# Attention followed by a squared-ReLU layer: where the score scale is applied, and which engine empties the value products

## The chip, the cores and the metric

The kernel runs on one core of one Trainium2 chip. The metric is the device time of one execution in microseconds; before the change it is 1281.25 us (median of 3 runs, 1281.09 to 1282.95). The engines are TensorE (PE for matmuls, PEld for its weight loads), VectorE (DVE), ScalarE (ACT), GpSimd (POOL) and SyncE (SP, which issues nearly all DMAs here). Each runs its own list of instructions in order; they meet through semaphores.

## What is computed

```python
# q, k, v: (8 batches, 8 heads, 576, 64), fp32; tau = 0.02
scores = (1 / 8) * q @ k.T
thresh = max(scores, axis=-1) - tau
scores = where(scores >= thresh, scores, -1e9)
attn   = exp(scores - max(scores, axis=-1))
attn   = attn / (sum(attn, axis=-1) + 1e-9)
x      = attn @ v                       # then (B, H, S, D) -> (4608, 512)
h      = maximum(x @ w_in, 0)           # w_in: (512, 2048), handed over as float64
out    = (h * h) @ w_out                # w_out: (2048, 512), float64 too
```

## The kernel before

The first 0.49 ms are attention, the rest the two matmuls of the feed-forward layer, which the change does not touch.

**Tiling of attention.** Two heads make a pair; there are 32 pairs. A *unit* is 128 rows of queries (or the two 64-row rests of two pairs) for both heads of a pair against all 576 keys; there are 144 units. The program runs in 72 *periods* (`period(p)`, p from -2 to 74, of which the outer ones are partial). Each scores and normalizes two units, A = 2p and B = 2p + 1, and multiplies the weights of the two units of p - 2 with the values.

**Operands.** Queries and keys are loaded by rows, turned by TensorE into PSUM (`turn`, L399; step `T`) and copied from there to SBUF by ScalarE (step `eT`). For an even turn these are a pair's 512 main queries (`qT`, two pieces of 256), for an odd one its 576 keys (`kT`, a piece of 256 and one of 320) and its 64 rest queries (`qR`). The pieces of queries are scaled on the way: the copy is an activation whose scale is the column `qscale` (L413). `qscale` is -1/8 in each partition, made from tau (L119), so that the scores come out negated and the maximum is a minimum. A pair is turned every second period: 62 turns fall on 62 periods, and of the periods from 3 on 14, 23, 32, 41, 50, 59 and 68 to 71 have none.

**One period.** The steps are written as lists of words (`PLAIN`, `CONVERTING`, `FIRSTS`, L606 to L622); each word issues its instructions, and so the list sets every engine's own order. Periods 3 to 34 use `CONVERTING`, since there the float64 weights are also taken apart into fp32 (c1 to c6, on ScalarE, VectorE and GpSimd); periods 35 to 71 use `PLAIN`; periods 0 to 2 have lists of their own. The words that matter:

- `SA`, `SB`: scores of A and B (L445), for each of 2 heads and 2 halves of 64 rows a matmul of 512 keys and one of the remaining 64, into PSUM.
- `topA1`, `topA0`, `topB1`, `topB0` (L463, VectorE): one maximum pass for each head. It reads 576 scores from PSUM, multiplies by 1.0, writes them to SBUF and gives their minimum in a second, small instruction (the accumulator's readout).
- `leastA`, `leastB` (L470, GpSimd): threshold; `powA1` and so on (L473, ScalarE): the exponential; `maskA1` and so on (L478, VectorE): the exponential times the comparison of the score with the threshold, which is a column with one value for each partition, and the sum.
- `over` (L485, GpSimd), `inv` (L488, VectorE), `spread` (L528, GpSimd): the reciprocal of the sums, widened for a transpose.
- `V`, `W`, `U` (L388): transposes of the weights; `eV`, `eW`, `eU` (L535, ScalarE): their copies to SBUF. `V` and `U` share one PSUM tile.
- `PV` (L544): the value products, 72 matmuls, into PSUM banks 0 (head 0) and 5 (head 1).
- `x` (L665, L667): VectorE multiplies head 0's product by the reciprocals on the way to SBUF, ScalarE copies head 1's; `xs` (L682): GpSimd multiplies head 1's by the reciprocals, and SP writes both to DRAM.

**Banks.** The scores fill PSUM banks 0 to 5. A's lie in banks 0, 1 and 4, 5, B's in 1, 2 and 3, 4. So `PV` follows A's two maximum passes, `T` (banks 1 and 4) follows B's, and the next `SA` follows `x` and `eT`. These waits between engines are worked out by `touch` (L363).

The plain list, which sets the order in the second half of attention:

```python
PLAIN = """
    fetch U SA topA1 over s1 topA0 SB topB1 inv sV eU powA1 idE V topB0 leastA spread PV powA0
    maskA1 leastB maskA0 eV T powB1 x maskB1 powB0 xs maskB0 eT W eW
""".split()
```

Of the kernel before, what the change touches and what calls it, by code (L numbers as in the profile page):

```python
# [10 lines left out]
FP32 = mybir.dt.float32  # L11
I32 = mybir.dt.int32
U32 = mybir.dt.uint32
ALU = mybir.AluOpType
# [34 lines left out]
def kernel(  # L49
# [25 lines left out]
    nc = tc.nc  # L75
    B, H, S, D = q.shape
    P = 128
# [260 lines left out]
    def places(i):  # L338
        if i not in turned:
            turned[i] = (  # L340
                sb.tile([P, MAIN], FP32, tag="qT", bufs=Q_RING, name="qT"),
                sb.tile([P, S], FP32, tag="kT", bufs=K_RING, name="kT"),
                sb.tile([P, REST], FP32, tag="qR", bufs=K_RING, name="qR"),
            )
        return turned[i]

# [52 lines left out]
    def turn(i, which, spots, other=None):  # L399

        nat, to = loaded.pop((i, which)), places(i)
        of = [nat[:, t, :] for t in range(FULL)] + ([loaded.pop((i, 2))] if which else [])
        for t, x in enumerate(of):
            for r, (spot, at) in enumerate(spots):
                rows = ds(r * HALF, HALF)
                made = nc.tensor.transpose(spot[:, ts(t, HALF)], x[rows, :], ident[rows, rows])  # L406
                touch("turns", made, at, BANK)
        half = FULL * HALF

        kind = "turned k" if which else "turned q"  # L410

        def scaled(to, spot):
            touch(kind, nc.scalar.activation(out=to, in_=spot[0], func=AF.Identity, scale=qscale[:, :]), spot[1], BANK, i)  # L413

        def then():
            part = lambda r, x, n: (spots[r][0][:, ds(x, n)], spots[r][1])
            if which:
                for r, n in ((0, half), (1, half + REST)):
                    spot = part(r, 0, n)
                    copy_by = other if r and other else nc.scalar.copy  # L420
                    touch(kind, copy_by(to[1][:, ds(r * half, n)], spot[0]), spot[1], BANK, i)
                scaled(to[2], part(0, half, REST))
                next_keys(i)
            else:
                for r in range(2):
                    scaled(to[0][:, ds(r * half, half)], part(r, 0, half))
                for n in later_loads(i, 0):
                    load_q(n)

        return then  # L430

# [2 lines left out]
    def scores(n, rest):  # L434

        of, t = units[n]
        at_k, count = (MAIN, REST) if rest else (0, MAIN)
        for j in range(2):
            first = n % 2 != j
            to = (3 * j + 1) * BANK + first * (BANK - REST) if rest else (3 * j + 2 * first) * BANK  # L440
            for c in range(2):
                rows, at = ds(j * D, D), ds(c * HALF, HALF)
                qT, kT, qR = turned[of[c]]
                lhs = qT[rows, ds((c * FULL + t) * HALF, HALF)] if t < FULL else qR[rows, :]
                made = nc.tensor.matmul(  # L445
                    sc[at, ds(to, count)], lhs, kT[rows, ds(at_k, count)], start=True, stop=True
                )
                touch("q scores" if t < FULL else "scores", made, to, count, of[c])

    def softmax(n):  # L450

        if n % 2 == 0:
            smalls[n // 2] = sb.tile([P, 4, 4], FP32, tag="small", bufs=4, name="small")
        small = smalls[n // 2]
        nmx, thr, sm = (small[:, i, ds(n % 2 * 2, 2)] for i in range(3))
        w = sb.tile([P, CH, 2, D], FP32, tag="w", bufs=4, name="w")
        s = sb.tile([P, 2, S], FP32, tag="s", bufs=2, name="s")
        weights[n] = w
        of = lambda j: s[:, j, :].rearrange("p (c d) -> p c d", d=D)

        def top(j):
            at = 3 * j * BANK + (n % 2 != j) * (2 * BANK - REST)
            made = nc.vector.tensor_scalar(  # L463
                out=s[:, j, :], in0=sc[:, ds(at, S)], scalar1=1.0, scalar2=None,
                op0=ALU.mult, op1=ALU.min, accum_out=nmx[:, j : j + 1],
            )
            touch("tops", made, at, S)

        def least():
            nc.gpsimd.tensor_scalar(out=thr, in0=nmx, scalar1=tau_p[:, :], scalar2=None, op0=ALU.add)  # L470

        def power(j):
            nc.scalar.activation(  # L473
                out=w[:, :, j, :], in_=of(j), func=AF.Exp, bias=nmx[:, j : j + 1], scale=-1.0
            )

        def mask(j):
            nc.vector.scalar_tensor_tensor(  # L478
                out=w[:, :, j, :], in0=of(j), scalar=thr[:, j : j + 1], in1=w[:, :, j, :],
                op0=ALU.is_le, op1=ALU.mult, accum_out=sm[:, j : j + 1],  # L480
            )

        def over():
            sm = small[:, 2, :]
            nc.gpsimd.tensor_scalar(out=sm, in0=sm, scalar1=1e-9, scalar2=None, op0=ALU.add)  # L485

        def inverse():
            nc.vector.reciprocal(out=small[:, 3, :], in_=small[:, 2, :])  # L488

        soft[n] = dict(top=top, least=least, power=power, mask=mask, over=over, inverse=inverse)  # L490
# [140 lines left out]
    def period(p):  # L631
# [26 lines left out]
        def given_out():  # L658
            if has(2 * m):
                x = sb.tile([P, 2, P], FP32, tag="x", bufs=2, name="x")  # L660
                by_vector = (0,)
                for j in range(2):
                    by = sc[:, ds(5 * j * BANK, P)], wT[m][:, ts(SCALE_AT + j, P)]
                    if j in by_vector:
                        made = nc.vector.tensor_tensor(out=x[:, j, :], in0=by[0], in1=by[1], op=ALU.mult)  # L665
                    else:
                        made = nc.scalar.copy(x[:, j, :], by[0])  # L667
                    touch("x", made, 5 * j * BANK, P, m)
                late["x"] = x, [j for j in range(2) if j not in by_vector], wT[m]
                wT.pop(m)  # L670
                valued(m)

        def scaled_x():
            if has(2 * m):
                x, js, by = late["x"]
                if len(js) == 2:
                    nc.gpsimd.tensor_tensor(
                        out=x[:, :, :].rearrange("p j q -> p (j q)"), in0=x[:, :, :].rearrange("p j q -> p (j q)"),
                        in1=by[:, ds(SCALE_AT * P, 2 * P)], op=ALU.mult,
                    )  # L680
                for j in js if len(js) == 1 else ():
                    nc.gpsimd.tensor_tensor(out=x[:, j, :], in0=x[:, j, :], in1=by[:, ts(SCALE_AT + j, P)], op=ALU.mult)  # L682
                give_x(m, x)
            ask(False)

# [669 lines left out]
```

## Time and profile before

| | |
|---|---|
| median of 3 runs | 1281.25 us |
| span of the profiled execution | 1278.6 us |
| attention, about | 0 to 493 us of the span |
| granted TensorE clock | 1.000 |
| PE busy | 1255.2 us (98%) |
| DVE busy | 1000.2 us (78%) |
| ACT busy | 855.6 us (67%) |
| POOL busy | 897.4 us (70%) |

In the profile's rows, a form such as `128x576 f32<-128x576 f32` is partitions by elements, out from in; `x288` is the count; behind `|` stand the busy time in us, the mean of one instruction in ns, and the idle time just before such instructions with the engine and line that ended it. In a timeline a row has start, duration, engine, line and operation; several like instructions in a row are merged (`x2`), and idle time before them stands in brackets. The records of ScalarE and VectorE overlap, since an instruction's record begins before the one in front has ended: the time that one takes from its engine is read from start to start, not from its duration.

### The profile page before, as it was taken

The page shows a single profiled execution, that of the slowest core. Times are in us where ns is not written, and L with a number is a line of the kernel's source. Part 1 is how long each engine was busy: PE and PEld are TensorE (multiplying, and loading weights), DVE is VectorE, ACT ScalarE, POOL GpSimd, SP SyncE. Part 2 cuts the span into 40 slices and gives each one's busy share as a digit, 9 for nine tenths or more (in the row PEclk, how much of TensorE's full clock was granted, in tenths as well). Part 3 has the DMA queues.
Part 4 walks back from the last instruction along what each step waited for, and adds up shares of the span by engine and source line. Part 5 has one row for each costly group of instructions (what it writes and reads, how often), then busy time and mean ns, then how long its engine had stood idle before and what let it go on. Part 6 is the DMA issues. An engine that isn't in the chain of part 4 may idle for free.

```text
span 1278.6 us, 44201 instructions
## 1 busy us (share of the span) xinstructions
PE 1255.2 (98%) x17459; PEld 1087.0 (85%) x17459; DVE 1000.2 (78%) x2449; ACT 855.6 (67%) x1552; POOL 897.4 (70%) x1094
## 2 busy tenths in 40 slices
PE   8999999999999999999999999999999999999998
PEld 6666666677777768988888888999999999999998
DVE  6999999999999997787878877877645664565463
ACT  6999999999999995666765767667422441343240
POOL 2565665655555557888798889858877777786775
PEclk9999999999999999999999999999999999999999
DMA  6566666544333413457666666589635414522511
GB/s 155 152 158 160 165 193 182 151 94 112 89 83 84 97 34 98 156 164 219 198 190 204 192 198 187 177 324 394 208 122 166 133 50 149 166 95 76 161 35 34
DMA packets 256591, 191.89 MB, mean 150 GB/s; under 512 B 96000, under 2 KB 217344, under 8 KB 256384
## 3 DMA queue, kind: packets, MB, share of 16 engines
q1 hardware_dynamic: 254928, 188.63, 49.8%
q8 instruction: 137, 2.24, 0.7%
q14 instruction: 70, 0.57, 0.1%
q10 hardware_dynamic: 1456, 0.44, 0.1%
HBM read 116.65 MB, written 72.35 MB: 148 GB/s over the span
## 4 chain that ended last, share of the span: by engine, by line
PE 70%; DMA 1%; ACT 1%; DVE 1%; issue 1%; ACTq 0%; DVEq 0%; SPq 0%
PE po L1085 30%; PE ph L946 27%; PE sc L544 5%; PE sc L445 4%; PE pt L388 2%; DMA wall<-w 1%; PE sc L406 1%; PE sc L388 1%; DVE arena L128 1%; DVE arena L463 0%; DMA g<-arena 0%; ACT arena L916 0%; ACT c L879 0%; DMA arena<-xT 0%; ACT arena L917 0%
## 5 line engine op out<-in xcount | busy, mean ns | idle before, releaser
L128 POOL TENSOR_TENSOR arena<-arena 128x512 f32<-128x512 f32 (+1 forms) x314 | 377.7, 1222 | 126.3 <-DVE arena L128 89.4
L1085 PE MATMUL po<-wall,arena 128*128 128x128 f32 x3528 | 394.4, 275 | 0.2 <-DVE arena L125 0.2
L1085 PEld LDWEIGHTS po<-wall,arena 128*128 128x128 f32 x3528 | 394.1, 192 | 0.4 <-DVE arena L125 0.4
L946 PE MATMUL ph<-arena,wall 128*128 128x128 f32 (+1 forms) x2352 | 387.4, 327 | 1.1 <-DVE arena L665 0.5
L946 PEld LDWEIGHTS ph<-arena,wall 128*128 128x128 f32 x2352 | 354.2, 191 | 34.2 <-DVE arena L128 2.2
L128 DVE TENSOR_TENSOR arena<-ph,arena 128x512 f32<-128x512 f32 x378 | 255.6, 688 | 75.8 <-PE ph L946 50.0
L125 POOL TENSOR_TENSOR arena<-arena 128x128 f32<-128x128 f32 (+2 forms) x314 | 255.2, 814 | 29.1 <-DMA arena<-w 10.7
L879 ACT COPY c<-arena 128x512 f32<-128x512 f32 (+2 forms) x319 | 176.1, 558 | 104.2 <-DVE arena L125 85.7
L473 ACT ACTIVATE arena<-arena 128x576 f32<-128x576 f32 x288 | 232.1, 918 | 16.7 <-DVE arena L463 16.7
L128 DVE TENSOR_TENSOR arena<-po,arena 128x128 f32<-128x128 f32 x378 | 108.3, 290 | 168.0 <-PE po L1085 167.4
L478 DVE SCALAR_TENSOR_TENSOR arena<-arena 128x576 f32<-128x576 f32 x288 | 225.5, 811 | 0.4 <-POOL arena L470 0.4
L463 DVE TENSOR_SCALAR_CACHE_REDUCE arena<-sc 128x576 f32<-128x576 f32 x288 | 204.5, 751 | 14.3 <-ACT arena L535 6.4
L125 DVE TENSOR_TENSOR arena<-arena,c 128x512 f32<-128x512 f32 (+2 forms) x283 | 176.8, 633 | 7.9 <-ACT c L879 6.1
L544 PEld LDWEIGHTS sc<-arena 64*64 64x64 f32 x5760 | 144.4, 133 | 43.1 <-DVE arena L463 39.1
L445 PE MATMUL sc<-arena 64*64 64x64 f32 (+1 forms) x2304 | 170.0, 415 | 0.3 <-DVE arena L665 0.3
L544 PE MATMUL sc<-arena 64*64 64x128 f32 (+1 forms) x5760 | 160.8, 262 | 8.5 <-DVE arena L463 5.8
L535 ACT COPY arena<-pt 128x1024 f32<-128x1024 f32 x144 | 166.0, 1153 | 1.6 <-PE pt L388 1.5
L769 ACT COPY arena<-po 128x128 f32<-128x128 f32 x63 | 16.6, 264 | 185.4 <-PE po L1085 185.4
L388 PEld LDWEIGHTS pt<-ident,arena 64*128 64x128 f32 x2304 | 83.0, 138 | 41.7 <-ACT arena L535 33.8
L388 PE MATMUL pt<-ident,arena 64*128 64x64 f32 x2304 | 100.8, 227 | 2.4 <-ACT arena L535 2.1
L445 PEld LDWEIGHTS sc<-arena 64*64 64x64 f32 x2304 | 62.5, 132 | 47.5 <-issue 22.7
L470 POOL TENSOR_SCALAR arena<-arena,tau_p 128x2 f32<-128x2 f32 x144 | 65.5, 455 | 41.8 <-DVE arena L463 35.2
(51 smaller groups left out, 936.6 us busy)
## 6 DMA issues: line engine op xcount, KB each, us to landing
g<-arena SPq DMA_DIRECT2D x144, 256.0 KB, 2.6
arena<-g SPq DMA_DIRECT2D x144, 256.0 KB, 4.5
w<-arena SPq DMA_DIRECT2D x60, 256.0 KB, 2.8
wall<-w SPq DMA_DIRECT2D x49, 256.0 KB, 5.3
arena<-w SPq DMA_DIRECT2D x44, 256.0 KB, 3.1
arena<-in_v_dram SPq DMA_DIRECT2D x32, 288.0 KB, 4.6
out_dram<-arena SPq DMA_DIRECT2D x70, 128.0 KB, 2.4
arena<-in_q_dram SPq DMA_DIRECT2D x64, 128.0 KB, 4.1
```

The source lines that it names most:

```text
L125: e.tensor_tensor(out=out, in0=x, in1=y, op=ALU.subtract)
L128: e.tensor_tensor(out=out, in0=x, in1=y, op=ALU.add)
L388: made = nc.tensor.transpose(pt[:, r, ts(slot, HALF)], of[rows, :], ident[rows, rows])
L445: made = nc.tensor.matmul(sc[at, ds(to, count)], lhs, kT[rows, ds(at_k, count)], start=True, stop=True)
L463: made = nc.vector.tensor_scalar(out=s[:, j, :], in0=sc[:, ds(at, S)], scalar1=1.0, scalar2=None, op0=ALU.mult, op1=ALU.min, accum_out=nmx ...
L473: nc.scalar.activation(out=w[:, :, j, :], in_=of(j), func=AF.Exp, bias=nmx[:, j : j + 1], scale=-1.0)
L478: nc.vector.scalar_tensor_tensor(out=w[:, :, j, :], in0=of(j), scalar=thr[:, j : j + 1], in1=w[:, :, j, :], op0=ALU.is_le, op1=ALU.mult, a ...
L535: touch("weights", nc.scalar.copy(joined(to), whole(pt, 0, count)), at, 2 * BANK, m)
L544: made = nc.tensor.matmul(sc[ds(u * D, D), ds(5 * j * BANK + row, count)], loaded_v[i][rows, (c - (u != j)) % CH, :], wT[m][rows, ds(weigh ...
L879: nc.scalar.copy(c, y)
L946: nc.tensor.matmul(to[:, j, :], W_IN[m, k][:, ts(h * parts_ + j, P)], x_of(m, k), start=(not more and j == 0), stop=True, skip_group_check ...
L1085: nc.tensor.matmul(to, g[:, j, :], w[:, j, :], start=(not more and j == 0), stop=(j == 3), skip_group_check=True)
```

## The change

The scale leaves the copies of the turned queries. Queries and keys are copied plainly; the 64 rest queries now lie behind the first 256 keys in `kT`, so that an odd turn is copied in two pieces of 320. The scores in PSUM are plain products, and the maximum pass multiplies them by the column `qscale` in place of the constant 1.0. The keys in `kT` are no longer in one run: a score matmul of 512 keys reads two runs of 256, 320 apart.

Both value products are copied to SBUF by ScalarE, and GpSimd scales both with one instruction of 256 columns; VectorE has no part in it any more.

```diff
@@ -338,9 +338,8 @@
     def places(i):
         if i not in turned:
             turned[i] = (
-                sb.tile([P, MAIN], FP32, tag="qT", bufs=Q_RING, name="qT"),
-                sb.tile([P, S], FP32, tag="kT", bufs=K_RING, name="kT"),
-                sb.tile([P, REST], FP32, tag="qR", bufs=K_RING, name="qR"),
+                sb.tile([P, 2, FULL * HALF], FP32, tag="qT", bufs=Q_RING, name="qT"),
+                sb.tile([P, 2, (FULL + 1) * HALF], FP32, tag="kT", bufs=K_RING, name="kT"),
             )
         return turned[i]
 
@@ -405,27 +404,16 @@
                 rows = ds(r * HALF, HALF)
                 made = nc.tensor.transpose(spot[:, ts(t, HALF)], x[rows, :], ident[rows, rows])
                 touch("turns", made, at, BANK)
-        half = FULL * HALF
-
-        kind = "turned k" if which else "turned q"
-
-        def scaled(to, spot):
-            touch(kind, nc.scalar.activation(out=to, in_=spot[0], func=AF.Identity, scale=qscale[:, :]), spot[1], BANK, i)
+        kind, n = "turned k" if which else "turned q", (FULL + (1 if which else 0)) * HALF
 
         def then():
-            part = lambda r, x, n: (spots[r][0][:, ds(x, n)], spots[r][1])
+            for r, copy_by in enumerate((nc.scalar.copy, other or nc.scalar.copy)):
+                touch(kind, copy_by(to[which][:, r, :], spots[r][0][:, 0:n]), spots[r][1], BANK, i)
             if which:
-                for r, n in ((0, half), (1, half + REST)):
-                    spot = part(r, 0, n)
-                    copy_by = other if r and other else nc.scalar.copy
-                    touch(kind, copy_by(to[1][:, ds(r * half, n)], spot[0]), spot[1], BANK, i)
-                scaled(to[2], part(0, half, REST))
                 next_keys(i)
             else:
-                for r in range(2):
-                    scaled(to[0][:, ds(r * half, half)], part(r, 0, half))
-                for n in later_loads(i, 0):
-                    load_q(n)
+                for n_ in later_loads(i, 0):
+                    load_q(n_)
 
         return then
 
@@ -434,17 +422,17 @@
     def scores(n, rest):
 
         of, t = units[n]
-        at_k, count = (MAIN, REST) if rest else (0, MAIN)
+        count = REST if rest else MAIN
         for j in range(2):
             first = n % 2 != j
             to = (3 * j + 1) * BANK + first * (BANK - REST) if rest else (3 * j + 2 * first) * BANK
             for c in range(2):
                 rows, at = ds(j * D, D), ds(c * HALF, HALF)
-                qT, kT, qR = turned[of[c]]
-                lhs = qT[rows, ds((c * FULL + t) * HALF, HALF)] if t < FULL else qR[rows, :]
-                made = nc.tensor.matmul(
-                    sc[at, ds(to, count)], lhs, kT[rows, ds(at_k, count)], start=True, stop=True
-                )
+                qT, kT = turned[of[c]]
+                lhs = qT[rows, c, ts(t, HALF)] if t < FULL else kT[rows, 0, ds(FULL * HALF, REST)]
+                keys = kT[rows, 1, ds(FULL * HALF, REST)] if rest else kT[rows, :, 0 : FULL * HALF]
+                to_ = sc[at, ds(to, count)] if rest else sc[at, ds(to, count)].rearrange("p (r n) -> p r n", r=2)
+                made = nc.tensor.matmul(to_, lhs, keys, start=True, stop=True)
                 touch("q scores" if t < FULL else "scores", made, to, count, of[c])
 
     def softmax(n):
@@ -461,7 +449,7 @@
         def top(j):
             at = 3 * j * BANK + (n % 2 != j) * (2 * BANK - REST)
             made = nc.vector.tensor_scalar(
-                out=s[:, j, :], in0=sc[:, ds(at, S)], scalar1=1.0, scalar2=None,
+                out=s[:, j, :], in0=sc[:, ds(at, S)], scalar1=qscale[:, :], scalar2=None,
                 op0=ALU.mult, op1=ALU.min, accum_out=nmx[:, j : j + 1],
             )
             touch("tops", made, at, S)
@@ -658,28 +646,17 @@
         def given_out():
             if has(2 * m):
                 x = sb.tile([P, 2, P], FP32, tag="x", bufs=2, name="x")
-                by_vector = (0,)
                 for j in range(2):
-                    by = sc[:, ds(5 * j * BANK, P)], wT[m][:, ts(SCALE_AT + j, P)]
-                    if j in by_vector:
-                        made = nc.vector.tensor_tensor(out=x[:, j, :], in0=by[0], in1=by[1], op=ALU.mult)
-                    else:
-                        made = nc.scalar.copy(x[:, j, :], by[0])
-                    touch("x", made, 5 * j * BANK, P, m)
-                late["x"] = x, [j for j in range(2) if j not in by_vector], wT[m]
+                    touch("x", nc.scalar.copy(x[:, j, :], sc[:, ds(5 * j * BANK, P)]), 5 * j * BANK, P, m)
+                late["x"] = x, wT[m][:, ds(SCALE_AT * P, 2 * P)]
                 wT.pop(m)
                 valued(m)
 
         def scaled_x():
             if has(2 * m):
-                x, js, by = late["x"]
-                if len(js) == 2:
-                    nc.gpsimd.tensor_tensor(
-                        out=x[:, :, :].rearrange("p j q -> p (j q)"), in0=x[:, :, :].rearrange("p j q -> p (j q)"),
-                        in1=by[:, ds(SCALE_AT * P, 2 * P)], op=ALU.mult,
-                    )
-                for j in js if len(js) == 1 else ():
-                    nc.gpsimd.tensor_tensor(out=x[:, j, :], in0=x[:, j, :], in1=by[:, ts(SCALE_AT + j, P)], op=ALU.mult)
+                x, by = late["x"]
+                flat = x[:, :, :].rearrange("p j q -> p (j q)")
+                nc.gpsimd.tensor_tensor(out=flat, in0=flat, in1=by, op=ALU.mult)
                 give_x(m, x)
             ask(False)
 
```

## The prediction, made before the changed kernel ran

> **What bounds the kernel now.** The diff touches only the attention part, so the table of stretches comes first. It gives the busy time of PE, PEld, DVE, ACT and POOL in each: periods 3 to 34, which also convert weights; periods 35 to 67; and the last four of attention.
>
> ```profile
> core 0: us, PE busy (x) PEld busy (x) DVE busy (x) ACT busy (x) POOL busy (x), PEclk, DMA share, GB/s
> 22.50:254.00 231.50, 219.23 (x5274) 153.53 (x5272) 228.45 (x659) 230.38 (x403) 138.24 (x229) 1.00 0.63 166
> 254.00:461.00 207.00, 205.56 (x5269) 149.43 (x5266) 198.73 (x593) 197.78 (x339) 114.60 (x199) 1.00 0.38 89
> 461.00:493.00 32.00, 30.31 (x840) 23.05 (x831) 30.15 (x85) 25.42 (x39) 16.18 (x29) 1.00 0.18 38
> ```
>
> Three engines are near full everywhere, so shares decide nothing. VectorE has 231.50 - 228.45 = 3.05 us to spare in 32 converting periods, 0.09 each; GpSimd is free for 40%. What sets a period must be read from its order. Here is one plain period in the timeline (start, duration), up to the start of the next value product (L544):
>
> ```profile
> 330.94 2.20 PE L544 MATMUL sc<-arena 64*64 64x128 f32 x72
> ...
> 332.22 0.82 DVE L478 SCALAR_TENSOR_TENSOR arena<-arena 128x576 f32<-128x576 f32 x1
> ...
> 332.96 0.81 DVE L478 SCALAR_TENSOR_TENSOR arena<-arena 128x576 f32<-128x576 f32 x1
> ...
> 333.71 0.28 DVE L665 TENSOR_TENSOR arena<-sc,arena 128x128 f32<-128x128 f32 x1
> 333.91 0.80 DVE L478 SCALAR_TENSOR_TENSOR arena<-arena 128x576 f32<-128x576 f32 x1
> ...
> 334.27 2.33 PE L445 MATMUL sc<-arena 64*64 64x512 f32 x32
> ...
> 335.74 0.76 DVE L463 TENSOR_SCALAR_CACHE_REDUCE arena<-sc 128x576 f32<-128x576 f32 x1 [0.27 <-ACT arena L535]
> 336.42 0.08 DVE L463 DVE_READ_ACCUMULATOR arena<-sc 128x1 f32 x1
> 336.42 0.75 DVE L463 TENSOR_SCALAR_CACHE_REDUCE arena<-sc 128x576 f32<-128x576 f32 x1
> ...
> 336.53 0.71 PE L388 MATMUL pt<-ident,arena 64*128 64x64 f32 x16
> ...
> 337.10 0.08 DVE L463 DVE_READ_ACCUMULATOR arena<-sc 128x1 f32 x1
> ...
> 337.23 2.20 PE L544 MATMUL sc<-arena 64*64 64x128 f32 x72
> ```
>
> The reader should see a ring. The value product writes banks 0 and 5, which hold unit A's scores until its two maximum passes (L463) have read them. The second pass ends its readout at 337.10 + 0.08 = 337.18, and the product starts 0.05 us later. The passes start when A's scores are in, and VectorE has stood idle 0.27 us before them. So the ring is value product, transposes, A's scores, two maximum passes, value product: 337.23 - 330.94 = 6.29 us. TensorE's other branch (V's transposes, L388 at 336.53) is only just covered. In the last period, where nothing waits, the product follows V's start by 0.64:
>
> ```profile
> 485.75 0.71 PE L388 MATMUL pt<-ident,arena 64*128 64x64 f32 x16
> 486.39 2.20 PE L544 MATMUL sc<-arena 64*64 64x128 f32 x72
> ```
>
> Here that would be 336.53 + 0.64 = 337.17, so the maximum passes are the later by 0.06 us: lengthening them counts in full, shortening them gains at most 0.06. The chain of waits (start, length) shows a period with transposed q or k and, from 349.77 on, one without:
>
> ```profile
> 343.47 2.20 PE sc L544 x72
> ...
> 349.77 2.19 PE sc L544 x72
> ...
> 352.86 2.15 PE sc L445 x29
> 355.02 0.69 DVE arena L463 x2
> 355.75 2.31 PE sc L544 x72
> ```
>
> After 337.23 the lengths are 6.24 and 6.30, and 5.98 without a turn. That last one passes through L463 in the chain itself, and is about VectorE's own sum: four passes, four masks (L478), L665 and a reciprocal.
>
> **The change, part by part.** Four groups of rows by shape (busy, mean ns) price the operations:
>
> ```profile
> L478 DVE SCALAR_TENSOR_TENSOR arena<-arena 128x576 f32<-128x576 f32 x288 | 225.5, 811 | 0.4 <-POOL arena L470 0.4
> L463 DVE TENSOR_SCALAR_CACHE_REDUCE arena<-sc 128x576 f32<-128x576 f32 x288 | 204.5, 751 | 14.3 <-ACT arena L535 6.4 <-PE sc L445 3.0 <-issue 2.1
> L237 DVE SCALAR_TENSOR_TENSOR arena<-arena 128x512 int32<-128x512 int32 x32 | 22.2, 693 | 0.0
> L665 DVE TENSOR_TENSOR arena<-sc,arena 128x128 f32<-128x128 f32 x72 | 20.5, 284 | 0.7 <-issue 0.5
> L413 ACT ACTIVATE arena<-sc,qscale 128x256 f32<-128x256 f32 x26 | 10.8, 469 | 0.0
> L421 ACT COPY arena<-sc 128x256 f32<-128x256 f32 x13 | 4.7, 363 | 0.0
> ```
>
> *The scale moves into the maximum pass.* L463's constant 1.0 becomes a column with one value for each partition. Before, the only VectorE instruction with such an operand is the mask. At the same 576 elements it takes 811 against 751 ns, 60 more; from start to start it is 332.96 - 332.22 = 0.74 against 337.10 - 336.42 = 0.68. L237 is the same operation with a constant: (693 - 284) / 384 = 1.07 ns an element over L665, so 761 at 576, 50 below the mask. The upper bound is ScalarE's difference for a column scale, 469 - 363 = 106 ns; the lower is nothing, if the mask pays for its blocks of 64. I take 0.06 us, VectorE's own row.
>
> Where it lies: two of the four passes are on the ring, 0.12 us a period. Of the 33 periods from 35 to 67, 30 have a turn: 30 x 0.12 = **+3.6 us**.
>
> *The value product leaves VectorE.* L665 goes: 333.91 - 333.71 = 0.20 us from start to start. In a plain period with a turn it is worth nothing, for it only widens the 0.27 us idle before L463. In one of the 7 without (three, and the last four) VectorE's sum counts: 4 x 0.06 - 0.20 = +0.04, together **+0.3 us**.
>
> *ScalarE.* It gains a second 128x128 copy and loses the column scale and one 64-wide instruction. A converting period in the timeline gives the lengths from start to start:
>
> ```profile
> 102.52 1.24 ACT L421 COPY arena<-sc 128x256 f32<-128x256 f32 x2
> 103.09 0.88 ACT L413 ACTIVATE arena<-sc,qscale 128x64 f32<-128x64 f32 x1
> 103.30 0.83 ACT L667 COPY arena<-sc 128x128 f32<-128x128 f32 x1
> 103.45 1.36 ACT L473 ACTIVATE arena<-arena 128x576 f32<-128x576 f32 x1
> ```
>
> The added copy is 103.45 - 103.30 = 0.15. Turned keys take 103.30 - 102.52 = 0.78 now and two copies of 320 later: 0.57 x 640 / 576 = 0.63, so -0.15. Turned queries lose 2 x 0.106 = 0.21. A k period changes by 0.00 and a q period by -0.06; a period without a turn gains 0.15, hidden by VectorE. The Trainium skill ("ScalarE: Activation LUTs", What ACT_TABLE_LOAD costs) gives about 93 ns for each such operand; by that figure q saves 0.19. In converting periods ScalarE's -0.03 on average meets VectorE's +0.04, of 0.09 spare. I take +0.01 x 32 = **+0.3 us**; the bounds are -0.06 x 32 = -1.9 and +0.04 x 32 = +1.3. Behind the second copy wait powB0, the evictions of turns and W, and then B's scores; they come 0.00 later (k) or 0.06 earlier (q). A's next scores (334.27) need both copies: the value product ends at 330.94 + 2.20 = 333.14, and even L665, behind two masks, is done by 333.99; two copies straight behind the product are earlier.
>
> *GpSimd* scales 256 columns instead of 128.
>
> ```profile
> L682 POOL TENSOR_TENSOR arena<-arena 128x128 f32<-128x128 f32 x72 | 35.9, 499 | 20.5 <-ACT arena L667 19.8 <-DMA arena<-in_k_dram 0.8
> L125 POOL TENSOR_TENSOR arena<-arena 128x384 f32<-128x384 f32 x4 | 4.0, 1007 | 0.3
> 335.56 0.23 POOL L485 TENSOR_SCALAR arena<-arena 128x4 f32<-128x4 f32 x1 [1.46 <-DVE arena L478]
> ```
>
> Halfway between these rows is 0.75 us, +0.25. The next instruction behind it, L485, is idle 1.46 us for the last mask, so it hides in plain periods; uncovered it would be 0.25 x 32 = 8 us in converting ones, but GpSimd's 40% covers it. SP issues the same DMAs to xT 0.25 later, and the query loads queued behind them slip likewise; their data is turned a period or more later.
>
> *Scores read keys as two runs of 256.* No moving operand here has two runs. ScalarE has an operand of that shape, and TensorE the same matmul at two widths:
>
> ```profile
> L445 PE MATMUL sc<-arena 64*64 64x512 f32 x1152 | 158.0, 613 | 0.3 <-DVE arena L665 0.3
> L445 PE MATMUL sc<-arena 64*64 64x64 f32 x1152 | 30.9, 218 | 0.0
> L535 ACT COPY arena<-sc 128x512 f32<-128x512 f32 x28 | 16.7, 596 | 0.0
> L769 ACT COPY arena<-ph 128x512 f32<-128x512 f32 x5 | 2.9, 585 | 6.7 <-PE ph L946 6.7
> ```
>
> ScalarE's copy of two runs (L535) takes 596 ns, of one run 585. The line through L445's rows, (613 - 218) / 448 = 0.88 ns a column, leaves 162 ns at no columns. A second start in each of the ring's two groups of four matmuls would be 30 x 2 x 0.16 = 9.7 us; below nothing there is no reason for, since the columns stay 512. I take nothing, by ScalarE's row of the same shape.
>
> *Ends.* In the first three periods each pass stands in line, 12 x 0.06 less one L665, about +0.4. At the end TensorE waits for both copies: +0.15, less what an earlier first score brings, **+0.5** together at most; I take +0.3.
>
> Sum: 3.6 + 0.3 + 0.3 + 0.3 = +4.5 us. The profiled span of 1278.6 becomes 1283.1; the median of the runs stands 2.65 above the span, which gives 1285.8.
>
> **The rivals.** *The column operand is free.* Then plain turn periods stay (the ring is unchanged), the 7 others gain at most 0.14 (TensorE's ring less the missing transposes, about 5.84), the converting ones 0.03 x 32 by ScalarE: -1.0 - 1.0 = -2.0, 1279.3. Its place is L463; it decides if that stays at 751 ns, and from 0.04 us a column down the change is within 0.2%. For it: its data is in PSUM, the mask's is not. Against: L237 and L665 agree with 751 at one slope; only the mask stands out. The Trainium skill ("VectorE: DVE Perf Modes", The TRN2 errata) prices a PSUM source at 120 cycles plus one an element, without a term for the operand: an estimate of 725 ns for 576, and 751 was measured; by it this rival holds.
>
> *The column costs ScalarE's 0.106.* The ring then pays 30 x 0.21 = 6.4, the 7 others 7 x 0.22 = 1.6, and the converting periods exceed VectorE's spare: 32 x (0.42 - 0.20 - 0.09) = 4.3. With 1.0 at the ends, +13.3: 1294.6.
>
> *GpSimd's longer product holds up the masks.* With L665 gone the masks are back to back, and each period's next mask waits the added 0.25: hidden by 0.27 in plain periods, 32 x (0.25 - 0.05) = 6.4 in converting ones, 1292. Against: masks average 811 although GpSimd works beside them. "SBUF — State Buffer" of the Trainium skill (SBUF: two separate sides) has such an exclusive lock; no row of L478 shows its price.
>
> *Two runs slow the matmul*: up to 9.7 more, 1295.5; its place is A's scores on the ring.
>
> **How the numbers follow.** The forecast has 0.62 (1283.4 to 1289, for 0.04 to 0.085 us a column), the free column 0.22, the other three 0.16 together. The range of 1279.0 to 1289.5 takes the forecast and most of the free column. Within 0.2% (2.6 us, what a measurement of this kernel can tell) lie 1278.7 to 1283.8: most of the free column and the forecast's low edge, 0.20. Slower gets 0.72. Faster, where the converting stretch gains its 1.9 as well, gets 0.08.
>
> **What would show it.** L463 near 811 ns and 0.74 from start to start; plain periods of 6.41 and 6.35; the value product still 0.05 behind the second pass; L478 unchanged; converting periods within 0.05; GpSimd's product near 0.75. The prediction is wrong if L463 stays at 751, if 64x512 matmuls lengthen, or if masks do.

## The result, and the profile after

The changed kernel takes 1293.15 us (median of 4 runs, 1292.1 to 1294.2) beside 1281.17 for the kernel before in the same comparison (1280.67 to 1282.95): a ratio of 1.009, 95% interval 1.0076 to 1.0105. That is 12 us slower; the forecast was 4.5, and the time lies above its range. The profiled span is 1291.4 us at a granted clock of 1.000. All of the loss lies in attention. The table of stretches of the changed kernel (columns as in the prediction; attention now ends near 505) and the last stretch of the kernel before:

```profile
22.50:254.00 231.50, 211.28 (x5226) 150.53 (x5218) 230.46 (x621) 229.54 (x419) 145.54 (x227) 1.00 0.62 163
254.00:470.00 216.00, 205.77 (x5256) 150.85 (x5256) 212.69 (x559) 200.36 (x353) 125.14 (x199) 1.00 0.37 86
...
505.00:1291.40 786.40, 781.69 (x5884) 748.26 (x5880) 530.43 (x1078) 390.11 (x753) 625.56 (x628) 1.00 0.52 166
```

```profile
493.00:1278.60 785.60, 781.23 (x5879) 747.82 (x5877) 530.28 (x1078) 389.80 (x751) 624.81 (x627) 1.00 0.52 166
```

The feed-forward stretch has nearly the same busy times on each engine. In the plain stretch VectorE has gone from 198.73 of 207.00 us busy (96%) to 212.69 of 216.00 (98%). To see where the time went, take the distance from every fourth start of the maximum pass (now L451, before L463) to the next fourth, which is one period, and add these up by stage (the last column is what was measured, after less before):

| periods | before, us | after, us | forecast's terms | measured |
|---|---|---|---|---|
| 0 to 2 | 19.16 | 20.22 | +0.4 | +1.06 |
| 3 to 34 | 224.98 | 227.61 | +0.3 | +2.63 |
| 35 to 67 | 207.77 | 215.96 | +3.7 | +8.19 |
| 68 to 70 | 18.05 | 19.34 | +0.2 | +1.29 |

The groups by shape of the changed kernel answer to rows of the prediction (L466 is the mask, L478 before; L435 the scores' matmul, L445 before):

```profile
L466 DVE SCALAR_TENSOR_TENSOR arena<-arena 128x576 f32<-128x576 f32 x288 | 242.0, 884 | 2.4 <-POOL arena L458 2.4
L451 DVE TENSOR_SCALAR_CACHE_REDUCE arena<-sc,qscale 128x576 f32<-128x576 f32 x288 | 219.8, 805 | 5.1 <-PE sc L435 3.0
...
L435 PE MATMUL sc<-arena 64*64 64x512 f32 x1152 | 157.0, 613 | 0.6 <-ACT arena L650 0.5
```

The maximum pass went from 751 to 805 ns, as forecast. The mask, which the change does not touch, went from 811 to 884: 16.5 us more, as much as the passes' 15.3. A plain period in the timeline (start, duration) shows which masks these are:

```profile
337.18 0.81 DVE L451 TENSOR_SCALAR_CACHE_REDUCE arena<-sc,qscale 128x576 f32<-128x576 f32 x1
...
337.92 0.80 DVE L451 TENSOR_SCALAR_CACHE_REDUCE arena<-sc,qscale 128x576 f32<-128x576 f32 x1
...
340.20 0.81 DVE L466 SCALAR_TENSOR_TENSOR arena<-arena 128x576 f32<-128x576 f32 x1
...
340.94 0.81 DVE L466 SCALAR_TENSOR_TENSOR arena<-arena 128x576 f32<-128x576 f32 x1
341.08 0.43 ACT L650 COPY arena<-sc 128x128 f32<-128x128 f32 x2
...
341.59 0.74 POOL L659 TENSOR_TENSOR arena<-arena 128x256 f32<-128x256 f32 x1 [0.43 <-ACT arena L650]
...
341.68 1.27 DVE L466 SCALAR_TENSOR_TENSOR arena<-arena 128x576 f32<-128x576 f32 x1
...
342.89 0.81 DVE L466 SCALAR_TENSOR_TENSOR arena<-arena 128x576 f32<-128x576 f32 x1
...
343.63 0.81 DVE L451 TENSOR_SCALAR_CACHE_REDUCE arena<-sc,qscale 128x576 f32<-128x576 f32 x1
```

The third mask starts 0.09 us after GpSimd's product (L659) and takes 342.89 - 341.68 = 1.21 us from start to start where its neighbours take 0.74. It then follows on at once, and the next maximum pass starts with no idle before it: the period is 343.63 - 337.18 = 6.45, and it is VectorE's own sum. The ring of the prediction no longer sets it. Each of the 33 periods from 35 to 67 has one such mask, of 1.22 on average, and all of them but the 45th, of which more below, read 6.44 to 6.55, with and without a turn.

In the converting stretch the product runs beside maximum passes, and it is the widening copy (L516, `spread`) that stands before a mask:

```profile
103.92 0.79 DVE L466 SCALAR_TENSOR_TENSOR arena<-arena 128x576 f32<-128x576 f32 x1
...
104.14 0.83 POOL L516 COPY arena<-arena 128x256 f32<-128x256 f32 x1
...
104.63 0.95 DVE L466 SCALAR_TENSOR_TENSOR arena<-arena 128x576 f32<-128x576 f32 x1
...
105.51 0.81 DVE L466 SCALAR_TENSOR_TENSOR arena<-arena 128x576 f32<-128x576 f32 x1
```

The same place before the change:

```profile
102.49 0.83 POOL L528 COPY arena<-arena 128x256 f32<-128x256 f32 x1
102.99 0.28 DVE L665 TENSOR_TENSOR arena<-sc,arena 128x128 f32<-128x128 f32 x1
...
103.19 0.81 DVE L478 SCALAR_TENSOR_TENSOR arena<-arena 128x576 f32<-128x576 f32 x1
...
103.93 0.81 DVE L478 SCALAR_TENSOR_TENSOR arena<-arena 128x576 f32<-128x576 f32 x1
```

Before, L665 stood between the two masks, the copy ended only 0.13 us after the start of the second (102.49 + 0.83 - 103.19), and that mask took 103.93 - 103.19 = 0.74. Now 0.34 us of the copy are left when the mask starts, and it takes 105.51 - 104.63 = 0.88.

One period stands out: the 45th is 9.08 us long (before 6.62). GpSimd waits there for data of the next stage, read back from DRAM:

```profile
320.46 0.54 SPq L814 DMA_DIRECT2D arena<-xT  x1
...
325.52 1.27 POOL L125 TENSOR_TENSOR arena<-arena 128x512 f32<-128x512 f32 x1 [3.57 <-DMA arena<-xT]
326.76 0.29 POOL L458 TENSOR_SCALAR arena<-arena,tau_p 128x2 f32<-128x2 f32 x1
...
327.10 0.92 DVE L466 SCALAR_TENSOR_TENSOR arena<-arena 128x576 f32<-128x576 f32 x1 [2.44 <-POOL arena L458]
```

The threshold (L458) is queued behind that sum, and VectorE stands idle 2.44 us for it. Before, the same sum started 3.04 us after its load was issued; here 5.06.

### The profile page after: what moved, and what is told of

Read it like the earlier page. It is cut to its first block, busy times and chain, and to the rows that moved or that the text cites. A ratio compares the mean times of both kernels' runs of the same rounds, so it can differ in the third digit from the quotient of the medians.

```text
span 1291.4 us, 44252 instructions
## 1 busy us (share of the span) xinstructions
PE 1249.5 (97%) x17459; PEld 1086.9 (84%) x17459; DVE 1021.0 (79%) x2377; ACT 860.3 (67%) x1592; POOL 918.2 (71%) x1094
## 4 chain that ended last, share of the span: by engine, by line
PE 61%; DMA 1%; DVE 1%; ACT 1%; issue 0%; ACTq 0%; DVEq 0%; SPq 0%
PE po L1062 30%; PE ph L923 28%; PE sc L532 2%; PE sc L435 1%; DMA wall<-w 1%; DVE arena L451 1%; DMA g<-arena 0%; ACT c L856 0%; ACT arena L893 0%; DVE arena L128 0%; PE pt L387 0%; PE sc L387 0%; ACT arena L894 0%; DVE arena L125 0%; PE sc L405 0%
## 5 line engine op out<-in xcount | busy, mean ns | idle before, releaser
L466 DVE SCALAR_TENSOR_TENSOR arena<-arena 128x576 f32<-128x576 f32 x288 | 242.0, 884 | 2.4 <-POOL arena L458 2.4
L461 ACT ACTIVATE arena<-arena 128x576 f32<-128x576 f32 x288 | 221.6, 821 | 22.3 <-DVE arena L451 22.2
L451 DVE TENSOR_SCALAR_CACHE_REDUCE arena<-sc,qscale 128x576 f32<-128x576 f32 x288 | 219.8, 805 | 5.1 <-PE sc L435 3.0
L435 PE MATMUL sc<-arena 64*64 64x64 f32 (+1 forms) x2304 | 169.2, 415 | 0.6 <-ACT arena L650 0.5
L523 ACT COPY arena<-pt 128x1024 f32<-128x1024 f32 x144 | 152.1, 1056 | 1.9 <-PE pt L387 1.7
L435 PEld LDWEIGHTS sc<-arena 64*64 64x64 f32 x2304 | 63.6, 133 | 45.1 <-issue 23.1
L894 ACT ACTIVATE arena<-arena 128x512 f32<-128x512 f32 x144 | 90.8, 630 | 4.6
```

What stands on the lines that cost most here:

```text
L435: made = nc.tensor.matmul(to_, lhs, keys, start=True, stop=True)
L451: made = nc.vector.tensor_scalar(out=s[:, j, :], in0=sc[:, ds(at, S)], scalar1=qscale[:, :], scalar2=None, op0=ALU.mult, op1=ALU.min, accu ...
L461: nc.scalar.activation(out=w[:, :, j, :], in_=of(j), func=AF.Exp, bias=nmx[:, j : j + 1], scale=-1.0)
L466: nc.vector.scalar_tensor_tensor(out=w[:, :, j, :], in0=of(j), scalar=thr[:, j : j + 1], in1=w[:, :, j, :], op0=ALU.is_le, op1=ALU.mult, a ...
L523: touch("weights", nc.scalar.copy(joined(to), whole(pt, 0, count)), at, 2 * BANK, m)
```

## Experiments

Two theories were set against each other: that the column operand cost more than its 0.06 us a pass, and that GpSimd held up VectorE's masks once L665 was gone. Lengths below are sums over the periods of a stage, as in the table. Each ratio is against the kernel before, run beside it.

**Each part alone.** First the scale in the maximum pass and the plain copies of turns, with the value products as before.

```diff
 def given_out():            # and scaled_x: the code of before
 ...
-                    touch("x", nc.scalar.copy(x[:, j, :], sc[:, ds(5 * j * BANK, P)]), ...)
+                    if j in by_vector:
+                        made = nc.vector.tensor_tensor(out=x[:, j, :], in0=by[0], in1=by[1], op=ALU.mult)
+                    else:
+                        made = nc.scalar.copy(x[:, j, :], by[0])
 ...
```

> Only the scale moves (plain copies of the turned queries and keys, the column operand in the maximum pass); the value products are emptied as before, head 0 by VectorE. Theory A (the column operand alone costs, on the ring and in VectorE's sum): the pass takes 0.74 from start to start; plain periods 6.41 and 6.35, about 6.22 without a turn; converting periods are VectorE's sum, 6.87 + 4 x 0.06 = 7.11; together some +9 us, 1288 to 1291, with no mask over 0.8. Theory B (GpSimd's 256-column product, running beside the masks, is what lengthened the kernel): the time is near before, 1280 to 1285, and all masks 0.74.

Then the other part: before's scores and turns, with the new value products.

```diff
 def given_out():            # and scaled_x: the code of the changed kernel
 ...
-                        made = nc.vector.tensor_tensor(out=x[:, j, :], in0=by[0], in1=by[1], op=ALU.mult)
+                    touch("x", nc.scalar.copy(x[:, j, :], sc[:, ds(5 * j * BANK, P)]), 5 * j * BANK, P, m)
 ...
```

> Only the value products move: both copied by ScalarE, both scaled by GpSimd in 256 columns; the scale stays in the copies of the queries and the maximum pass keeps its constant. Theory B (a mask that starts while GpSimd runs its product is held until that ends): one mask in four takes 1.2 in plain periods, the pass stays at 0.68; plain periods about 6.3, without a turn 5.98 - 0.20 + 0.47 = 6.25; converting periods are ScalarE's, 0.15 longer; 1285 to 1290. Theory A: masks stay 0.74, periods without a turn fall to about 5.84, converting ones still pay ScalarE's 0.15: 1283 to 1285.

The groups of the stretch from 255 to 470 us, of the first kernel and then of the second:

```profile
L466 DVE SCALAR_TENSOR_TENSOR arena<-arena 128x576 f32<-128x576 f32 x135 | 104.7, 811 | 0.5 <-POOL arena L458 0.5
...
L451 DVE TENSOR_SCALAR_CACHE_REDUCE arena<-sc,qscale 128x576 f32<-128x576 f32 x133 | 102.4, 807 | 5.3 <-issue 3.9 <-PE sc L435 0.7
```

```profile
L478 DVE SCALAR_TENSOR_TENSOR arena<-arena 128x576 f32<-128x576 f32 x132 | 115.3, 921 | 2.7 <-POOL arena L470 2.3 <-ACT arena L473 0.3
...
L463 DVE TENSOR_SCALAR_CACHE_REDUCE arena<-sc 128x576 f32<-128x576 f32 x132 | 93.7, 747 | 5.5 <-PE sc L445 1.7 <-ACT arena L535 1.5 <-ACT arena L473 0.3
```

Scale only: 1292.47 us, ratio 1.0084 (1.0066 to 1.0102). Masks stay at 811, and plain periods are 6.42, 6.35 and 6.23 as the ring and VectorE's sum have it; converting ones 7.11. Products only: 1291.33, ratio 1.0069 (1.0045 to 1.0092). The passes stay at 747, the masks have 921. So the long masks come with the value products and not with the column, and each part alone costs nearly what both cost together; in the second's profile 2.1 us of this are a longer period 45 (8.68 beside 6.62). Both times lie somewhat above the ranges given for them. With the scale alone, the periods 3 to 34 lose 4.0 us: VectorE's sum grows by 4 x 0.06 = 0.24 with L665 still there, and it is idle for only 0.2 us in all 32. What follows period 70 was 2.5 us longer in that profile than before, which stays unexplained.

**No product, and half a product.** The first leaves GpSimd's multiplication out, so that the value products are not normalized; the second multiplies only head 0's 128 columns and leaves head 1's unnormalized.

```diff
-                nc.gpsimd.tensor_tensor(out=flat, in0=flat, in1=by, op=ALU.mult)
+                nc.gpsimd.tensor_tensor(out=x[:, 0, :], in0=x[:, 0, :], in1=by[:, 0:P], op=ALU.mult)   # second only
```

> The changed kernel with GpSimd's product left out, so that the value products are written unscaled. Theory B: no mask over 0.8 in plain periods; these fall from 6.45 to 6.41, 6.35 and 6.03 without a turn; converting periods stay at 7.05, since there the widening copy, not the product, meets a mask; 1285 to 1288. Rival C (masks lengthen because they now follow each other with no other VectorE work between): masks of 1.2 and 6.45 us remain, 1292 to 1294.

> The changed kernel with GpSimd scaling head 0's 128 columns alone; head 1's value product is written unscaled. Theory B in a dose: the product shrinks from 0.74 to 0.46, so the held mask shrinks by the same 0.28, from 1.21 to 0.93; VectorE's sum in plain periods is then 6.0 + 0.19 = 6.2, below the ring: 6.41 and 6.35, about 6.2 without a turn; 1286 to 1289. If the hold has a fixed price: masks of 1.2 and 6.45.

Without the product: 1288.24, ratio 1.0051 (1.0033 to 1.007), 0.2 above the range given; the masks of the plain stretch average 813 ns, no mask there takes more than 0.85, and periods are 6.41, 6.35 and 6.02:

```profile
L466 DVE SCALAR_TENSOR_TENSOR arena<-arena 128x576 f32<-128x576 f32 x135 | 102.7, 813 | 0.0
```

With half: 1289.0, ratio 1.0048 (1.0033 to 1.0063). The timeline of the half product:

```profile
346.06 0.68 POOL L658 TENSOR_TENSOR arena<-arena 128x128 f32<-128x128 f32 x1 [0.22 <-ACT arena L650]
...
346.36 1.01 DVE L466 SCALAR_TENSOR_TENSOR arena<-arena 128x576 f32<-128x576 f32 x1
...
347.29 0.08 DVE L466 DVE_READ_ACCUMULATOR arena<-arena 128x1 f32 x1
```

The mask behind it takes 347.29 - 346.36 = 0.93: between 0.74 with no product and 1.21 with the full one; in the 33 plain periods such a mask takes 0.94 on average. The hold grows with GpSimd's instruction. The product's record of 0.68 is longer than the 0.46 that 128 columns take where nothing is in their way, for it begins in the middle of the mask in front and is itself held until that has ended: what counts for the next mask is how much of the product is left then, 0.38 here and 0.65 with 256 columns.

**The product one period later, whole.** In plain periods the product moves to the front of the next period, beside the maximum passes. The output is complete.

```diff
-    fetch U SA topA1 over s1 topA0 SB ...
-    ... x maskB1 powB0 xs maskB0 eT W eW
+    fetch U SA topA1 over s1 xs topA0 SB ...
+    ... x maskB1 powB0 maskB0 eT W eW        # x, xs: a deque hands the tile on to the next period
```

> The changed kernel, but in plain periods GpSimd scales the value products one period later, behind its first short instructions, when VectorE runs maximum passes (scores from PSUM) and no masks. Nothing is left out. Theory B: masks 0.74, plain periods 6.41 and 6.35, converting ones 7.05: 1285 to 1288, like the kernel without the product. Rival C: masks of 1.2 remain, 1292 to 1294. Rival D (GpSimd has too much work and is late with thresholds): masks 0.74, but VectorE idle before them and periods over 6.45.

```profile
340.63 0.82 DVE L451 TENSOR_SCALAR_CACHE_REDUCE arena<-sc,qscale 128x576 f32<-128x576 f32 x1 [0.35 <-ACT arena L523]
...
341.91 0.73 POOL L661 TENSOR_TENSOR arena<-arena 128x256 f32<-128x256 f32 x1
...
346.98 0.82 DVE L451 TENSOR_SCALAR_CACHE_REDUCE arena<-sc,qscale 128x576 f32<-128x576 f32 x1 [0.29 <-ACT arena L523]
```

1287.78 us, ratio 1.0047 (1.003 to 1.0063), 5.4 below the changed kernel with the same work (7.0 above the kernel before where that is 12.0 above). The product takes its 0.73 beside passes, which read PSUM, and neither is slowed; the masks of the stretch average 811 again, and none takes more than 0.75. VectorE is idle 0.3 us before the pass: the ring sets the period, 346.98 - 340.63 = 6.35. The plain stage is 210.92 us, +3.15 over before, and the last three periods 18.24, +0.19: close to the forecast's +3.7 and +0.2. In these two stages the forecast was right for this kernel, not for the one it was made for; the first 35 periods lose 3.5 here too.

**The widening copy earlier too.** On top of this, in converting periods `inv` and `spread` go before the masks.

```diff
-    ... topB0 over topB1 powA0 c4 powB0 PV eT inv leastA maskA1 x powB1 leastB spread V eV ...
+    ... topB0 over inv topB1 powA0 spread c4 powB0 PV eT leastA maskA1 x powB1 leastB V eV ...
```

> The kernel with the late product (column kept, nothing left out), and in converting periods the reciprocal and GpSimd's widening copy go ahead of the second maximum pass of B, so that the copy runs beside passes and not beside a mask. Theory B (any GpSimd instruction that reads SBUF holds up a mask that starts during it): no mask over 0.8 in converting periods, which fall from 7.04 to 6.9 to 7.0; 1283 to 1287. If VectorE's sum there is set by something else: masks of 0.88 or periods of 7.04 stay, 1287 to 1288.5.

A miss: 1295.1, ratio 1.0105 (1.009 to 1.012). No converting mask takes more than 0.8 any more, but a converting period is 7.32 us, for the reciprocal now waits for GpSimd:

```profile
101.98 1.48 POOL L248 TENSOR_TENSOR wall<-arena 128x512 int32<-128x512 int32 x1 [2.82 <-DVE arena L237]
...
103.42 0.72 POOL L661 TENSOR_TENSOR arena<-arena 128x256 f32<-128x256 f32 x1
...
104.12 0.61 POOL L221 TENSOR_SCALAR arena<-arena 128x512 f32<-128x512 f32 x1
...
104.81 0.23 POOL L473 TENSOR_SCALAR arena<-arena 128x4 f32<-128x4 f32 x1
...
105.08 0.18 DVE L476 RECIPROCAL arena<-arena 128x4 f32<-128x4 f32 x1 [0.29 <-POOL arena L473]
```

The sums for the reciprocal (L473, step `over`) stand behind two conversions (L248, L221) and the product on GpSimd's list. What the copy's hold costs in converting periods is so not shown by taking it away.

**No column.** A constant in the column's place; it leaves out a negative tau, for which the column would have another sign. Once in the changed kernel, once with the value products as before, once with the late product.

```diff
-                out=s[:, j, :], in0=sc[:, ds(at, S)], scalar1=qscale[:, :], scalar2=None,
+                out=s[:, j, :], in0=sc[:, ds(at, S)], scalar1=-SCALE, scalar2=None,
```

> The changed kernel with the constant -1/8 in the maximum pass in place of the column, which leaves out the case of a negative tau. Column theory: the pass returns to 0.68, VectorE's sum falls by 4 x 0.06, converting periods become ScalarE's (6.9 to 7.06, 6.81 by VectorE), plain ones about 6.3 with masks of 1.2 still there, about 6.2 without a turn; 1281 to 1285. If the two runs of keys, not the column, cost the time: 1290 or more.

> As the scale-only kernel (value products as before), but with the constant -1/8, so that ScalarE's plain copies are all that is left of the change; leaves out a negative tau. Column theory: pass 0.68, masks 0.74, converting periods VectorE's 6.87 for ScalarE has 6.90 and 6.77, plain periods 6.29, 6.23 and 5.98 as before the change: 1276 to 1280, below the kernel before. If plain copies or the two runs cost something: 1281 or more.

> The changed kernel with the constant -1/8 (leaves out a negative tau) and in plain periods the GpSimd product one period later, beside the maximum passes. Both costs are then gone from plain periods: 6.29 and 6.23 by the ring, 5.8 to 5.9 without a turn; converting periods ScalarE's, 6.95 to 7.05: 1278 to 1282. If either cost had another cause, plain periods stay above 6.35 and the time above 1284.

The groups of the first, from 255 to 470 us:

```profile
L466 DVE SCALAR_TENSOR_TENSOR arena<-arena 128x576 f32<-128x576 f32 x136 | 120.7, 936 | 1.1 <-POOL arena L458 1.0
...
L451 DVE TENSOR_SCALAR_CACHE_REDUCE arena<-sc 128x576 f32<-128x576 f32 x135 | 95.5, 743 | 1.0 <-issue 0.3
```

They take 1283.69 (ratio 1.0023, 1.0011 to 1.0034), 1280.27 (0.999, 0.998 to 0.9999) and 1280.51 (0.9993, 0.9984 to 1.0003). The pass is back at 743 to 747 ns in all three: the 0.06 us is the operand's and nothing else's. The second time is 0.3 above the range given, the others lie within theirs. The held masks stay in the first, but cost it little: without the column VectorE's sum is 6.31, where the ring was 6.29 and 6.23. Between the scale alone and its twin with a constant lie 12.2 us, of which 9.7 fall on the periods (479.19 against 469.45 from 0 to 70), since VectorE still has L665 to do; between late products with and without the column 7.3.

**The stall of period 45.** The sum that waits for its load goes one period later: in the changed kernel, in the one before, and in the one with a constant and before's value products, which leaves out a negative tau as above.

```diff
-                if p == X_FIRST + 4:
+                if p == X_FIRST + 5:
```

> The changed kernel with the sums of the first set of activations begun one period later, so that they do not wait for a load that has just been issued. If the one period of 9.08 us (before: 6.62) is that wait, it becomes 6.45, no GpSimd wait for that load over 0.5 us remains, and the time falls by 2 to 3 us: 1290 to 1291. If it is a matter of chance elsewhere: some other long period, 1292 to 1294.

> The kernel before with the same delay of those sums. The wait there was 1.5 us and its period 6.62 against 6.3: 0.3 less, 1280 to 1281.5; within the noise of the kernel before.

> Plain copies, the constant -1/8 in the maximum pass (leaves out a negative tau), value products as before, and the delayed sums. Its period 45 took 8.45 us without the delay; with 6.3 there: 1276.5 to 1279, below the kernel before by 0.2% to 0.35%. If that wait is chance: 1279 to 1281.

Changed kernel: 1292.19 us, ratio 1.0073 (1.006 to 1.0087), period 45 at 6.44, profiled span 1288.7, 2.7 less. Before: 1281.4, ratio 0.9994 (0.9985 to 1.0003). With the constant: 1279.41, ratio 0.9974 (0.9964 to 0.9985), the only version clearly below the kernel before. In the profile the stall is worth 2.7 us, in the medians of the changed kernel 1.0 and beside the kernel before 2.1 (9.9 above it where it was 12.0), and the runs overlap (1290.5 to 1294.2 against 1292.1 to 1294.2). The first and the last time lie above the ranges given, by 1.2 and 0.4. How long the load takes differs from kernel to kernel; period 45 was 6.30 to 9.08 us without this edit, and why was not settled.

## Why the prediction was wrong

**The ring, and the column at 0.06 us: right.** From start to start the pass takes 337.92 - 337.18 = 0.74 (before 0.68). Where no mask is held, plain periods are 6.41 and 6.35, to the hundredth as forecast. "VectorE: DVE Perf Modes" of the Trainium skill (The TRN2 errata) has no term for such an operand, and an estimate by its table is 725 ns for the pass with either. The trace does not agree: 751 with the constant, 805 with the column, so the free column did not come.

**Two runs of keys: right.** The 64x512 matmul stayed at 613 ns (L435), and the kernel with a constant and before's value products, which keeps the two runs, takes no longer than the kernel before.

**GpSimd's product: the length right, the place wrong.** It takes 0.74 (forecast 0.75). The step that failed is "so it hides in plain periods", and with it the price of the rival: "each period's next mask waits the added 0.25: hidden by 0.27 in plain periods". Two things were missed. First, L665 itself was the cover. Another period of the kernel before shows it:

```profile
314.37 0.52 POOL L682 TENSOR_TENSOR arena<-arena 128x128 f32<-128x128 f32 x1 [0.38 <-ACT arena L667]
...
314.50 0.28 DVE L665 TENSOR_TENSOR arena<-sc,arena 128x128 f32<-128x128 f32 x1
314.70 0.80 DVE L478 SCALAR_TENSOR_TENSOR arena<-arena 128x576 f32<-128x576 f32 x1
...
315.43 0.81 DVE L478 SCALAR_TENSOR_TENSOR arena<-arena 128x576 f32<-128x576 f32 x1
```

The product had ended at 314.89, 0.19 us after the mask's start, and the mask took 0.73. "Masks average 811 although GpSimd works beside them" was read as evidence against a hold; but this mask had hardly overlapped with the product. With L665 gone the mask starts 0.20 earlier, and the product ends 0.25 later: 0.45 together, and 0.47 was measured. Nor was the trace before without held masks: where the product began later, as in periods 42, 51 and 60, its mask took 0.83 to 0.84, against the prediction's "no row of L478 shows its price":

```profile
301.83 0.46 POOL L682 TENSOR_TENSOR arena<-arena 128x128 f32<-128x128 f32 x1 [0.55 <-ACT arena L667]
...
302.00 0.91 DVE L478 SCALAR_TENSOR_TENSOR arena<-arena 128x576 f32<-128x576 f32 x1
302.84 0.08 DVE L478 DVE_READ_ACCUMULATOR arena<-arena 128x1 f32 x1
```

Second, the 0.27 us of VectorE's idle time was spent twice: the four columns take 0.24 of it. VectorE's sum, 5.98 in the turn-free period before, becomes 5.98 + 0.24 - 0.20 + 0.47 = 6.49 (measured 6.45) and passes the ring's 6.41 and 6.35. The turn-free periods, three in the plain stage and three of the four at the end that the table holds, lose 0.38 to 0.46 each where +0.04 was forecast. Worked through with the right hold, the sum would have been 4.5 + 30 x (6.49 - 6.38) + 7 x (6.49 - 6.02) = 11.1 us. That this is near the measured 12 is partly luck: it puts 3.7 + 3.3 + 1.4 = 8.4 in the plain stage, where 5.7 was measured without period 45, since a period reads 6.45 and some before already read 6.36 to 6.64; and it leaves +0.3 in the converting stage.

That the product is what holds the mask is shown: without it, with half of it, and with all of it elsewhere the mask takes 0.74, 0.93 and 0.74 instead of 1.21, in every one of the 33 periods (but for 0.85 without it in period 45, where the widening copy comes late). The rival had been placed in the converting periods; there the product runs beside maximum passes and holds nothing.

**Converting periods: forecast +0.3, measured +2.6.** Two steps failed. "Of 0.09 spare" is an average: before, in the 11 periods of 6.87 to 6.93 VectorE is never idle, and in the others, most of 7.01 to 7.11, it is idle for up to 0.15. And the hold by the widening copy, 0.88 - 0.74 = 0.14, was not in the sum. VectorE's sum, 6.87 in the short periods, becomes 6.87 + 0.24 - 0.20 + 0.14 = 7.05: passes, L665, hold. Of the 32 periods 25 now read 7.04 or 7.05, and in 28 VectorE is never idle; each has one held mask. Raising the shorter periods of before to 7.05 makes 2.0 of the 2.6 us; the rest lies in a few longer periods, which vary from kernel to kernel. The hold costs this only together with the column: with a constant in the column's place and the holds still there, the stage takes 225.05, as before (224.98). What it costs with the column is argued from the sum; the experiment that took it away put another wait in its place.

**Ends.** The first three periods lose 1.06, not 0.4. Without the product they lose 1.04, so GpSimd's product is not the cause; the scale alone costs 0.58 there and the products alone 0.45. Which wait makes the second part was not tried. The last three lose 1.29, of which 1.1 is the hold (0.19 without it).

**Period 45** is 2.5 us of the profile's difference that no step foresaw. It is the wait for a load, and it varies; whether the change has a part in it is not shown.

**Each part alone.** That both parts together cost no more than one has its reason in the bounds: the scale alone fills VectorE in converting periods (7.11; it is idle for 0.2 us in all 32), the products alone fill ScalarE there (6.92 to 7.29 in most; idle for 0.6 us in all, VectorE for 7.7), with one copy of 0.15 more while the scaled copies stay, and together each gives back a part of the other's (7.05).

## What to carry to other kernels

Before an instruction is taken from an engine, look in the timeline at what runs on the other engines beside it: it may be the only thing between two instructions that cannot run together, and its time is then not saved. A mean over a group says nothing against a hold unless the rows show that the two did overlap. Idle time of an engine can be spent only once: add up all edits on that engine's own list and set the sum against the ring, before each is called hidden.

## What the runs showed of the hardware

**A mask waits for GpSimd.** The mask has two inputs in SBUF. When a GpSimd instruction that reads SBUF has begun first, the mask ends late by what is left of that instruction at the mask's start, less about 0.18 us: 342.33 - 341.68 - 0.18 = 0.47 (measured 0.47) in the changed kernel, 346.74 - 346.36 - 0.18 = 0.20 (0.19) with the half product, 104.97 - 104.63 - 0.18 = 0.16 (0.14) behind the widening copy. In the 14 profiles kept, 452 masks of more than 0.80 us agree with this sum within 0.03 us. Which record begins first decides only roughly: 32 further masks were held for 0.56 to 0.59 although the product's record began 0.02 to 0.04 after theirs, and in the changed kernel and the one with the products alone, where it began 0.07 to 0.08 after, it was the product that waited (1.32 to 1.34). It also holds the other way: the copy, 0.40 us in plain periods, where it runs beside a maximum pass, takes 0.83 where it begins beside a mask, and the product takes 1.25 where the mask began 0.16 earlier, in the kernel with the products alone:

```profile
336.82 0.81 DVE L478 SCALAR_TENSOR_TENSOR arena<-arena 128x576 f32<-128x576 f32 x1
...
336.98 1.25 POOL L671 TENSOR_TENSOR arena<-arena 128x256 f32<-128x256 f32 x1 [0.67 <-ACT arena L662]
```

Maximum passes, with one input and that in PSUM, were neither held nor did they hold in these rows. "SBUF — State Buffer" of the Trainium skill (SBUF: two separate sides) says that a VectorE instruction with two SBUF inputs and a GpSimd instruction that reads SBUF take a shared pair of ports as an exclusive lock, whole instructions at a time. These rows agree, as if the first 0.18 us of a mask did not need the lock.

**A column operand has a price on VectorE:** 0.06 us in a pass of 576 elements from PSUM (0.738 against 0.678 from start to start), the same step that the mask showed before the change.
